# Memory-augmented attention in 64 dependent segments: column-tiled PV and P transposes, 4-byte block transposes, re-cut Wo rows, and 20 streamed weight pieces in place of 21

## The chip, the cores and the metric

One core of one Trainium2 chip. The metric is the device time of one execution in microseconds (us), as the median of several runs. Every profiled and timed run in this document was in the fast state; the granted TensorE clock, averaged over a run, was 0.98 to 0.99 in all of them. These averages are not as alike as they look; the section on the result says why.

## The reference, cut to what matters

```python
# S=2048, Dm=640, H=32 heads, Dh=192, M=8 memory rows, seg_len=32 -> 64 segments
def attention(x, mem0, Wq, Wk, Wv, Wo):
    mask = (idx[:, None] < M) | (idx[:, None] >= idx[None, :])       # 40 x 40
    mem = mem0
    for s in range(64):
        h = concat([mem, x[:, 32*s:32*s+32]], axis=1)                # 40 rows
        q, k, v = (einsum('btd,dhe->bhte', h, W) for W in (Wq, Wk, Wv))
        p = softmax(where(mask, q @ k.T * Dh**-0.5, -1e9))
        o = einsum('bhte,hed->btd', p @ v, Wo)
        mem = o[:, :M]                     # the next segment starts from it
        outs.append(o[:, M:])

b   = (gelu(x @ w_gate) * (x @ w_up)) @ w_down
g   = sigmoid((x * gate_w).sum(-1, keepdims=True))
out = g * a + (1 - g) * b                  # a: the attention's output
```

The eight memory rows make the 64 segments a chain. Nothing of segment s + 1 that touches the memory can start before the last Wo product of segment s is done. All of Wq, Wk, Wv and Wo (84 pieces in this kernel) is used in every segment.

## The kernel before

The FFN and the projections of the last 8 rows of each segment's input ("left") are done first, in some 316 us. Then come 64 segments. A segment works through four octets of eight heads. The program below is TensorE's order: `q`, `k`, `v` are projections (five pieces each), `sc` scores, `ex` the softmax on ScalarE and VectorE, `pt` the transpose of P, `pv` P times V, `wo` the output projection, `tq` and `tk` block transposes of Q and K on VectorE.

```python
PROG = [("q", 0), ("tq", 0), ("k", 0), ("tk", 0), ("v", 0),
        ("q", 1), ("sc", 0), ("tq", 1), ("k", 1), ("ex", 0), ("tk", 1), ("v", 1),
        ("q", 2), ("pt", 0), ("sc", 1), ("tq", 2), ("k", 2), ("ex", 1), ("tk", 2), ("pv", 0), ("v", 2),
        ("q", 3), ("pt", 1), ("sc", 2), ("tq", 3), ("ex", 2), ("k", 3), ("tk", 3), ("pv", 1), ("v", 3),
        ("pt", 2), ("sc", 3), ("pw", 0), ("ex", 3), ("wo", 0), ("pv", 2), ("pw", 1), ("wo", 1, 0), ("pt", 3),
        ("wo", 1, 1), ("wo", 1, 2), ("pv", 3), ("wo", 2), ("wo", 3)]
```

The weights do not all fit on chip. A Q, K or V piece has 384 KB (3072 bytes a partition), a Wo piece 320 KB. Two pieces are held in PSUM, most are resident in SBUF, and the rest is **streamed again in every segment** through five buffers. SyncE issues the loads in order; each waits until the buffer it goes into has been consumed. Which pieces stream is chosen so that they are spread evenly over the segment, by a cost model of TensorE's time:

```python
nstream = 0
while True:
    streamed = set()
    for k in range(nstream):
        target = (k + 0.5) * tseg / nstream
        best = min((i for i in range(npieces) if i not in streamed and i not in held_i), key=lambda i: abs(tcons[i] - target))
        streamed.add(best)
    if tot_bytes - GO - GQ - sum(piece_size(order[i]) for i in streamed) <= res_cap:
        break                                    # ends at 21 here
    nstream += 1
```

The operations that the change and the argument touch:

```python
def cmode(s, m, o, bank):                        # q, k: 5 pieces x 4 matmuls, 128x32 column tiles
    ...
    act: activation(out=rows_sb[m], in_=ps[:, bank, 0:384], func=Copy)            # rows evac
def row_transp(s, m, o):
    dve: transpose(out=dst[:, :, 0:L], in_=rows_sb[m])                            # 384 2-byte elements
def v_oct(s, o):
    left = s % 4 == 0                            # every 4th segment also makes Vl for four segments
    ...
def softmax(s, o):
    ...                                          # exp (ScalarE), sum and reciprocal (VectorE), then P:
    dve: tensor_tensor(out=pm_sb, in0=S3[:, :, 0:L], in1=rcb, op=mult)
         tensor_tensor(out=pl_sb[:, :, M*q:M*q+M], in0=S3[:, :, L:R], in1=rcb, op=mult)
def p_transp(s, o):                              # two full-width transposes
def pv_oct(s, o):
    pe: pair(A, 0, W, 0, 0, 1) + pair(A, W, W, 256, 1, 2)     # 4 full-width (128x128) matmuls
    pe: 4 matmuls in 64-column tiles                          # the middle chunk
    act: uT evac (two chunks)      dve: uT mid (one chunk)
def segment(s):
    ...                                          # PROG, then the hand-over:
    dve: mrow = ps[OB]                           # mem rows
    dve: rowb = ps[OB] * gate + rowb             # mix
    pe:  memT (6 matmuls)          dve: mem evac          # next segment may start
```

## Time and profile before

| | before |
|---|---|
| time, median of the first 3 runs | 1992.56 us (1985.2 to 1994.85) |
| profiled run | 1984.8 us |
| TensorE busy, of the span | 92% |
| DMA packet time per engine in an ordinary segment | 24.3 us of 25.14, 0.967 |
| period of a segment: Vl (s % 4 = 0) / ordinary (1, 2) / the one before Vl (3) | 26.79 / 25.14 / 25.73 us |

The periods are distances between the memory transposes of one segment and the next, read from the start times of all matmuls in the trace and averaged over 62 periods. The packet time is the sum of the durations of all DMA packets in these periods over 16 engines. The prediction shows the sums and windows behind the last rows. What it doesn't show are the lines that the experiments came to turn on. First two groups of the page (busy us, mean ns of one | idle time before): the ScalarE eviction of Q and K rows and VectorE's transpose behind it.

```profile
L929 DVE STREAM_TRANSPOSE arena<-arena 128x384 bf16<-128x384 bf16 x512 | 292.4, 571 | 136.1 <-ACT arena L924 135.9
L924 ACT ACTIVATE arena<-ps 128x384 bf16<-128x384 f32 x512 | 250.7, 490 | 308.3 <-PE ps L920 258.1
```

Then the waits view (who waits, on what: us in all, times, longest). TensorE's weight loads at the Q/K projections and at the P transposes wait for VectorE's product that makes P (L1002): 54 us over all lines. Waits for the stream are of the same size, 67 us, most of them for Q; those for Wo are a small part.

```profile
PEld ps L920 <- DMA arena<-in_A_Wq_dram: 35.8, 77, 1.4
...
PEld ps L920 <- DVE arena L1002: 26.0, 46, 2.2
PEld ps L1010 <- DVE arena L1002: 17.6, 39, 1.0
...
PEld ps L1064 <- DMA arena<-in_A_Wo_dram: 9.5, 23, 1.5
```

The first row for L1002 is written at a projection, which does not read P. I count it to the P transpose, which stands next in TensorE's program: in the start times the wait is a gap ahead of the last matmul of a Q block: 0.10 us in the third, 0.27 in the fourth, with 0.05 elsewhere some 0.45 us in an ordinary segment.

Last, TensorE's timeline at the start of segment 0, where V waits for the left half of x:

```profile
328.66 3.07 PE L939 MATMUL ps<-arena 128*32 128x384 bf16 x36 [9.97 <-DMA arena<-left_xt_scratch]
```

### The profile page before, as it was taken

How to read it: one execution, taken by the hardware profiler on the slowest of the kernel's cores; microseconds unless marked ns; L12 is line 12 of the kernel's file. 1: busy time of each engine (PE TensorE's matmuls, PEld its weight loads, DVE VectorE, ACT ScalarE, POOL GpSimd, SP SyncE). 2: the span in 40 equal slices, each digit the busy share in tenths (PEclk: the TensorE clock that was granted, in tenths of full speed). 3: DMA queues.
4: the chain of work that ended last, by engine and by line, in shares of the span. 5: the costliest groups of instructions: out<-in, count | busy, mean ns of one | idle time of the engine just before them, and what ended most of it. 6: DMA issues, size and time to landing. Idle time of an engine off the chain costs nothing.

```text
span 1984.8 us, 74702 instructions
## 1 busy us (share of the span) xinstructions
PE 1833.7 (92%) x32125; PEld 1092.4 (55%) x32125; DVE 1052.9 (53%) x3210; ACT 804.2 (41%) x1917; POOL 146.5 (7%) x547
## 2 busy tenths in 40 slices
PE   7899994899999999999999999999999999999998
PEld 3454442555565555555555555555555555556555
DVE  3222332456565656555555565656555555556565
ACT  2222221344444444444444444444444444444444
POOL 0000000000000000000000000000000000000000
PEclk9999996999999999999999999999999999999999
DMA  9411468999999999999998999999999999999998
GB/s 370 162 46 60 130 155 279 315 311 318 322 312 322 316 327 313 316 317 323 310 330 288 322 312 317 311 327 309 315 311 323 314 320 313 313 324 318 328 312 284
DMA packets 356327, 576.27 MB, mean 290 GB/s; under 512 B 83474, under 2 KB 240666, under 8 KB 355994
## 3 DMA queue, kind: packets, MB, share of 16 engines
q1 hardware_dynamic: 276922, 531.99, 79.8%
q10 hardware_dynamic: 79072, 39.50, 7.2%
q8 instruction: 251, 4.11, 0.8%
q14 instruction: 82, 0.67, 0.1%
HBM read 550.25 MB, written 21.10 MB: 288 GB/s over the span
## 4 chain that ended last, share of the span: by engine, by line
PE 73%; DMA 14%; DVE 5%; ACTq 5%; ACT 2%; issue 2%; SPq 0%; DVEq 0%
PE ps L1064 20%; PE ps L920 18%; PE ps L939 10%; DMA arena<-in_A_Wq_dram 5%; PE ps L842 4%; PE ps L968 3%; DMA arena<-in_A_Wo_dram 3%; PE ps L775 3%; PE ps L772 3%; PE ps L1030 2%; DMA arena<-in_A_Wk_dram 2%; PE ps L1044 2%; PE ps L960 2%; ACTq L666 2%; ACTq L857 2%; PE ps L790 2%
## 5 line engine op out<-in xcount | busy, mean ns | idle before, releaser
L920 PE MATMUL ps<-arena 128*32 128x384 bf16 x10240 | 527.0, 329 | 53.0 <-DVE arena L1123 21.2
L1064 PE MATMUL ps<-arena 128*40 128x320 bf16 x6144 | 466.6, 300 | 4.8 <-DMA arena<-in_A_Wo_dram 3.9
L924 ACT ACTIVATE arena<-ps 128x384 bf16<-128x384 f32 x512 | 250.7, 490 | 308.3 <-PE ps L920 258.1
L920 PEld LDWEIGHTS ps<-arena 128*32 128x32 bf16 x10240 | 252.4, 96 | 222.4 <-DMA arena<-in_A_Wq_dram 35.8
L929 DVE STREAM_TRANSPOSE arena<-arena 128x384 bf16<-128x384 bf16 x512 | 292.4, 571 | 136.1 <-ACT arena L924 135.9
L1064 PEld LDWEIGHTS ps<-arena 128*40 128x40 bf16 x6144 | 297.5, 100 | 102.9 <-DMA arena<-in_A_Wo_dram 9.5
L939 PE MATMUL ps<-arena 128*32 128x384 bf16 x6400 | 318.2, 329 | 12.4 <-DMA arena<-left_xt_scratch 10.0
L939 PEld LDWEIGHTS ps<-arena 128*32 128x32 bf16 x6400 | 162.7, 97 | 110.3 <-DMA arena<-left_xt_scratch 10.4
L599 ACT ACTIVATE arena<-ps 128x576 bf16<-128x576 bf16 (+1 forms) x192 | 114.3, 595 | 224.6 <-PE ps L1064 197.5
L900 POOL COPY arena<-arena 128x96 bf16<-128x96 bf16 x256 | 69.0, 270 | 1618.3 <-PE ps L968 851.6
L950 ACT ACTIVATE arena<-ps 128x384 bf16<-128x384 f32 x256 | 125.8, 492 | 133.8 <-PE ps L939 98.9
L1048 ACT ACTIVATE arena<-ps 128x320 bf16<-128x320 f32 x256 | 111.8, 437 | 130.2 <-PE ps L1032 130.1
L997 DVE TENSOR_REDUCE arena<-ps 104x4 f32<-104x160 f32 x256 | 82.1, 321 | 146.4 <-ACT ps L995 146.2
L1013 DVE TENSOR_TENSOR arena<-ps,arena 128x320 bf16<-128x320 bf16 x256 | 124.6, 487 | 35.5 <-PE ps L1011 30.7
L1108 DVE CAST arena<-ps 104x320 bf16<-104x320 f32 x63 | 31.0, 492 | 190.1 <-PE ps L1064 190.1
L995 ACT ACTIVATE ps<-ps 104x160 f32<-104x160 f32 x256 | 73.4, 287 | 118.5 <-DVE ps L985 77.2
L968 PE MATMUL ps<-arena 128*40 128x40 bf16 (+1 forms) x4096 | 120.7, 181 | 0.4
L612 ACT ACTIVATE arena<-ps 128x256 bf16<-128x256 bf16 x320 | 102.2, 386 | 36.5 <-DVE arena L1016 14.0
L1052 DVE CAST arena<-ps 128x160 bf16<-128x160 f32 x256 | 77.8, 304 | 72.1 <-PE ps L1044 69.1
L983 DVE TENSOR_REDUCE arena<-ps 104x4 f32<-104x160 f32 x256 | 80.8, 316 | 60.3 <-PE ps L968 60.0
L842 PE MATMUL ps<-arena 128*128 128x512 bf16 x480 | 104.3, 379 | 2.8 <-ACT arena L849 2.8
L968 PEld LDWEIGHTS ps<-arena 128*40 128x40 bf16 (+1 forms) x4096 | 99.2, 96 | 11.4 <-DVE arena L929 2.0
(75 smaller groups left out, 1702.5 us busy)
## 6 DMA issues: line engine op xcount, KB each, us to landing
arena<-in_A_Wo_dram SPq DMA_DIRECT2D x528, 320.0 KB, 4.5
arena<-in_A_Wk_dram SPq DMA_DIRECT2D x404, 384.0 KB, 4.7
arena<-in_A_Wq_dram SPq DMA_DIRECT2D x341, 384.0 KB, 4.5
arena<-in_A_Wv_dram SPq DMA_DIRECT2D x146, 384.0 KB, 5.0
left_qk_scratch<-arena ACTq DMA_DIRECT2D x16, 768.0 KB, 7.9
arena<-left_qk_scratch ACTq DMA_DIRECT2D x64, 192.0 KB, 4.7
arena<-in_A_x_dram SPq DMA_DIRECT2D x4, 640.0 KB, 15.2
xt_scratch<-arena ACTq DMA_DIRECT2D x4, 640.0 KB, 9.1
```

Source lines behind the costliest of these rows:

```text
L599: S_.add("act", lambda e: e.activation(out=bview(o_held2, GQ)[:, c0:c1], in_=psb(b)[:, p0:p0 + c1 - c0], func=ACTF.Copy), reads=[r_ps[b]], ...
L612: S_.add("act", lambda e, b=b: e.activation(out=flat[:, 256 * b:256 * b + 256], in_=psb(b)[:, 768:1024], func=ACTF.Copy), reads=[r_ps[b]], ...
L842: S_.add("pe", [lambda e, k=k, g_=gs[k][0], i=i, bk=bk: e.matmul(ps[:, bk, 0:NL].rearrange("p (g t) -> p g t", t=L), g_[:, i * 128:(i + 1) ...
L920: S_.add("pe", [lambda e, j=j, k=k, gv=gv: e.matmul(ps[32 * j:32 * j + 32, bank, 0:384].rearrange("p (c i) -> p c i", i=32), Hb[hb][:, k, ...
L924: S_.add("act", lambda e: e.activation(out=rows_sb[m], in_=ps[:, bank, 0:384], func=ACTF.Copy), reads=[r_ps[bank]], writes=[r_rows[m]], na ...
L929: S_.add("dve", lambda e: e.transpose(out=dst[:, :, 0:L], in_=rows_sb[m].rearrange("p (c r) -> p c r", r=L)), reads=[r_rows[m]], writes=[r ...
L939: return [lambda e, j=j: e.matmul(ps[32 * j:32 * j + 32, bk, 0:384], lhs, g_[:, 384 * j:384 * (j + 1)], start=(k == 0), stop=(k == KT - 1) ...
L950: S_.add("act", lambda e: e.activation(out=v_sb[o % NVB], in_=ps[:, bank, 0:384], func=ACTF.Copy), reads=[r_ps[bank]], writes=[r_v[o % NVB ...
L968: fns.append(lambda e, gp=gp, lo=lo, hi=hi, i=3 * tl + c, tl=tl, last=(c == 1): e.matmul(ps[gp:gp + R, bank, tl * R:(tl + 1) * R], Qs[lo:h ...
L1013: S_.add("dve", lambda e: e.tensor_tensor(out=PTm, in0=apx(pv[:, 0:104], [[64, 2], [0, 4], [1, R]]), in1=apx(mbd, [[0, 2], [1, 4], [0, R]] ...
L1048: S_.add("act", lambda e: e.activation(out=apx(u[:, 0, 0, :], [[2 * R, 2], [3 * R, 4], [1, R]]), in_=ps[:, A, 0:2 * W].rearrange("p (c t r ...
L1064: fns.append(lambda e, g_=g_, i=i, c=c, h=h, tl=tl, cc=cc, u=u: e.matmul(ps[64 * h:64 * h + R, OB, 0:HD], u[:, tl, cc, :], g_[:, i, HD * h ...
```

## The change

Its intent is to shorten both things that run near full: fewer streamed bytes in larger packets for the DMA engines, and fewer changes of tiling for TensorE. VectorE is relieved along the way. The diff, cut to its core:

```diff
-    wsA["rowb"] = al(HD * 2)
-    wsA["mrow"] = al(HD * 2)                      # 1280 bytes a partition freed ...
+    o_rowb, o_mrow = wsB_off["v"] + 768, wsB_off["v"]   # ... by overlaying both on the V buffers
 # Wo rows by threes: a partition's two rows are adjacent in DRAM unless p % 3 == 1
-            return Wo2[:, 2 * key[1]:2 * key[1] + 2, :]
+            r0, r1 = wo_row(2 * key[1]), wo_row(2 * key[1] + 1)      # wo_row(c) = 384*(c//3) + c%3
+            return bass.AP(Wo2.tensor, Wo2.offset + r0 * Dm, [[3 * Dm, 128], [(r1 - r0) * Dm, 2], [1, Dm]])
+    def may_stream(key):
+        return key[1] % 3 != 1 if key[0] == 3 else key[0] != 2 or key[1] >= 2
 # exp is put ahead of the next k block (PROG), COST gets new numbers, tseg = tt + 1.4
 # Q/K rows: pairs of 2-byte elements, transposed as 4-byte ones
-        act: activation(out=rows_sb[m], in_=ps[:, bank, 0:384], func=Copy)
+        act: activation(out=rows_sb[m].rearrange("p (b i h) -> p b h i", b=6, h=2), in_=..., func=Copy)
-        dve: transpose(out=dst[:, :, 0:L], in_=rows_sb[m])
+        dve: transpose(out=dst[:, :, 0:L], in_=rows_sb[m].bitcast(F32))
 # Vl of octets 0 and 1 is made at the end of the segment before
-        left = s % 4 == 0
+        left = s % 4 == 0 and (s == 0 or o >= 2)
 # P in one product for octets 0 to 2; P transposes in column tiles
-        dve: pm_sb = S3[:, :, 0:L] * rcb ; pl_sb[..] = S3[:, :, L:R] * rcb
+        dve: p_sb[0:104, :, 0:R] = S3 * rcb                        # o < 3; o = 3 as before
+        pe:  8 transposes in 32-column tiles (o < 3), 4 in 64-column tiles (o = 3)
 # PV
-        pe: pair(A, 0, W, 0, 0, 1) + pair(A, W, W, 256, 1, 2)      # full width
+        pe: for cc in 3 chunks, for left in (False, True), for h in 2 halves: one 64-column tile
-        dve: uT mid
+        act: uT mid (o < 2)      dve: uT mid (o >= 2)
 # hand-over
-        mem rows, mix, memT, mem evac
+        mem rows, [Vl of o0 ahead], memT, [Vl of o1 ahead], mem evac, mix      # [..] if (s+1) % 4 == 0
 # b_load moves from k2 to behind the last pv (its buffer is V's now);
 # the eight gate copies move from ScalarE's DMA queue, late, to SyncE's, early
```

The mask is now two 64x64 tiles and the scores begin with the 64-row ones. The selection loop ends with 20 streamed pieces, 8 of Wo and 12 of Q, K and V.

> **What bounds the kernel now.** I read the sums of the page first, then the chain of waits for the period of a segment, then windows of single segments, then TensorE's timeline in two segments.
>
> The page, busy tenths in 40 slices: TensorE and the DMA engines are both nearly full from the eighth slice on, so no single row decides.
> ```profile
> PE 1833.7 (92%) x32125; PEld 1092.4 (55%) x32125; DVE 1052.9 (53%) x3210; ACT 804.2 (41%) x1917; POOL 146.5 (7%) x547
> ...
> PE   7899994899999999999999999999999999999998
> ...
> DMA  9411468999999999999998999999999999999998
> ...
> q1 hardware_dynamic: 276922, 531.99, 79.8%
> ```
> Some 316 us are the FFN, the left projections and set-up; the rest is 64 dependent segments. The memory transpose (L1119) marks each end. Its 63 groups run from 364.9 to 1957.5 us: 62 periods, 25.69 us each. The chain of waits gives the single starts: most segments take 24.5 to 25.6 us, every fourth (the one that also projects Vl) 26.7. Segment 0 takes 49.8 us.
>
> Windows (columns: length, busy time of PE, weight loads, DVE, ACT, POOL, granted clock, DMA share, GB/s): the first is a Vl segment, the next two ordinary ones, the last two lie in segment 0.
> ```profile
> 955.00:981.00 26.00, 25.20 (x518) 15.96 (x510) 16.51 (x51) 11.31 (x28) 2.15 (x8) 1.00 0.93 304
> ...
> 981.15:1005.77 24.62, 23.32 (x454) 14.29 (x454) 14.62 (x47) 11.45 (x28) 2.16 (x8) 1.00 0.98 331
> ...
> 1005.77:1030.57 24.80, 23.51 (x454) 14.33 (x454) 14.73 (x47) 11.19 (x28) 2.16 (x8) 1.00 0.97 326
> ...
> 316.00:328.50 12.50, 2.70 (x45) 1.25 (x44) 1.16 (x2) 2.45 (x5) 0.00 (x0) 0.64 0.82 263
> 328.50:340.00 11.50, 10.63 (x190) 5.88 (x194) 4.17 (x13) 3.93 (x7) 1.44 (x6) 0.73 0.64 215
> ```
> The ordinary segment is bound by DMA (0.97 to 0.98). The Vl segment is bound by TensorE: its timeline has hardly a gap. Vl is four times 20 matmuls at 0.82 us, 3.28 us, so TensorE alone needs 26.7 - 3.3 = 23.4 us for an ordinary segment and loses 1.3 to 2.2 us there. The cause is the stream: counts of the DMA issues give (1419 weight issues - 75 at the start) / 64 = 21 pieces a segment, 8 of Wo and 13 of Q, K, V.
>
> TensorE's timeline of one ordinary segment (start, duration; I count from start to start):
> ```profile
> 1004.94 0.47 PE L1119 MATMUL ps<-arena 128*128 128x8 bf16 x6 [0.59 <-DVE arena L1108]
> 1005.77 1.81 PE L920 MATMUL ps<-arena 128*32 128x384 bf16 x40 [0.36 <-DVE arena L1123]
> 1007.41 0.99 PE L939 MATMUL ps<-arena 128*32 128x384 bf16 x20
> 1008.22 0.99 PE L920 MATMUL ps<-arena 128*32 128x384 bf16 x20
> 1009.13 0.25 PE L960 MATMUL ps<-arena 128*40 128x160 bf16 x2
> 1009.22 0.46 PE L968 MATMUL ps<-arena 128*40 128x40 bf16 x16
> 1009.61 1.00 PE L920 MATMUL ps<-arena 128*32 128x384 bf16 x20
> ...
> 1025.28 0.24 PE L1030 MATMUL ps<-arena 128*128 128x160 bf16 x1
> ...
> 1025.58 0.29 PE L1044 MATMUL ps<-arena 128*64 128x160 bf16 x4
> 1025.70 1.52 PE L1064 MATMUL ps<-arena 128*40 128x320 bf16 x20
> ```
> A Q block takes 0.82 us ahead of another 32-column block and 0.91 ahead of the mask: a change of the array's tiling costs about 0.1 us. The segment hand-over idles TensorE 0.59 + 0.36 = 0.95 us.
>
> **What the Trainium skill says.** TensorEngine Tiling (Array Packing), Key Properties: changing the tiling mode drains TensorE. The 0.1 us above agrees. TensorE: Matmul & The Clock Gate, part 1: starts of small matmuls are never closer than about 25 ns. The 16 score matmuls take 0.39 us, 24 ns each: agrees. DMA: Bandwidth & Descriptors, Why small descriptors are slow: a fixed cost per packet. In the trace's packet records a 1280-byte packet takes 63.1 ns (mean), a 3072-byte one 142.9: 50.5 against 47.6 ns per KB, so it agrees but is small. Vector Engine (DVE) Microarchitecture Reference, 3.8: the 32x32 transpose passes one element per cycle per lane. The trace can't show its 4-byte case yet; its VectorE evictions of 160 and 384 elements took 304 and 544 ns, 1.07 ns an element, and the 384-element transpose 571 ns, so a pace of one element at a time fits.
>
> **The change, part by part.**
>
> (1) *Streamed bytes.* The 1280 bytes per partition of the b and memory rows are freed and let one more Q/K/V piece stay: by the selection loop's arithmetic 20 pieces, 8 of Wo and 12 of Q, K, V. One piece is 128 packets x 142.9 ns / 16 engines = 1.14 us. Wo rows by threes make the two rows that a partition gets adjacent for all pieces allowed to stream, so 256 packets of 1280 bytes become 128 of 2560. By a line through the two means a 2560-byte packet takes 120 ns, against 2 x 63.1 = 126: 8 x 128 x 6 / 16 = 0.39 us. All packets between 420 and 1950 us took 1460.5 us per engine; over 59.6 periods that is 24.5 us a segment. After: 24.5 - 1.14 - 0.39 = 23.0 us. At the share that an ordinary segment reaches now (0.97) it needs **23.7 us**.
>
> (2) *TensorE in a segment.* PV now: beside the 32-column blocks 0.1 in, 0.30 for the four full-width matmuls with a switch, 0.12 for the four tiled ones, 0.1 out, 0.62; beside Wo 0.1 + 0.30 + 0.12 = 0.52 (Wo has the same tiles). After: three groups like the tiled one, 0.36, with 0.1 + 0.1 beside the blocks and none beside Wo. Saved 2 x 0.06 + 2 x 0.16 = 0.44 us. P transposes 0 to 2: a drain less (0.1), but eight small ones at 25 ns in place of two take 0.1 more: nothing. The last P transpose, beside Wo: 0.1 + 0.19 becomes four at 25 ns: 0.19 saved. The reordered scores let the last octet pass to Wo without a switch: 0.1. Sum 0.73: an ordinary segment needs **22.7 us** of TensorE.
>
> (3) *Vl for octets 0 and 1 ahead.* 1.64 us leave the Vl segment and go to the end of the segment before, where they fill 0.95 us of hand-over. So TensorE needs 22.7 + 1.64 = **24.3** in the Vl segment and 22.7 + 0.69 = **23.4** in the one before.
>
> (4) *VectorE and ScalarE.* A 4-byte transpose has 192 elements fewer: 571 - 192 x 1.07 = 366 ns, 8 x 0.2 = 1.6 us saved. Joined P products: 3 x (291 + 181 - 333) = 0.42 us. Two mid evictions of 304 ns go to ScalarE, which has 13 us free. VectorE falls from 14.7 to some 12.1 us. All lies beside other work; only the waits for the P product (L1002: about 15 us of PE idle in all, mostly inside DMA slack) shrink.
>
> (5) *Segment 0.* V waited 10 us for the left x load, which sat in ScalarE's queue behind the eight gate copies (9.5 us). These move to SyncE's queue, long before. But that segment also loads late residents: the windows of its 50 us add up to 43 us of DMA at full share. So I take 6 us of the 10.
>
> (6) *Set-up otherwise* (mask halves, zeroing, later memory load): under 1 us on the path.
>
> Sum: of four segments, two ordinary at 23.7, the Vl one at 24.4, the one before it at 23.9 (both bounds near each other cost a little): mean 23.9 against 25.69. 63 x 1.79 = 113 us, plus 6: 1992.6 - 119 = 1873. I put the prediction at **1872 us**.
>
> **The rivals.** *A: the overlays become waits.* The b rows may be loaded only after the last PV (some 4.9 us before the segment's end), and ScalarE must first evict and issue (0.44 + 0.8 us); the load took 4.6 us to land. So it lands about 1 us after the end, and the mix sits in VectorE's queue ahead of the next Q transpose, due 1.6 us after the start. For: there is no room to spare. Likewise V's second eviction must wait for the out stores (issued 2 to 3.6 us into the segment, 4.0 us to land), 1 to 2 us later than now. Against: both have 1 to 3 us until TensorE needs them. If they bite, 0.3 to 0.6 us a segment: about 1900. *B: the DMA is limited by bytes alone.* If larger packets gain nothing the ordinary segment needs 24.1: mean 24.2, 1893. For: the rate per byte differs only 6% between sizes. *C: the strided reads are slow.* The V weights now step three elements and Q/K two. If weight loads there took twice their 100 ns, PV would save nothing; TensorE would have 23.1, still under the DMA: about 1880. *D: better than summed.* With TensorE further from binding, queues refill sooner, share 0.99 and 0.2 us less PE: mean 23.3, 1835.
>
> **Range and chances.** The path gets shorter in every part and both bounds fall by 5 to 6% or more, so less than 2% (over 1952.7) would need new waits of over 1.2 us a segment. Range 1838 to 1915. Faster 0.94, within 2% 0.05, slower 0.01.
>
> **What would show it right or wrong.** Right: 20 pieces a segment, packets of 2560 bytes near 120 ns; period near 23.9 us with DMA share still 0.96 to 0.97 in ordinary segments; the Vl segment within 1 us of the others; PV beside Wo 0.36 us from start to start; transpose near 366 ns; no left-x wait in segment 0, which takes about 44 us. Wrong: TensorE waiting for the Q or K transpose behind the mix, ScalarE waiting for the out stores with TensorE behind it, the DMA share well under 0.95 (then TensorE or a hand-over binds), or transposes no shorter.

## The result, and the profile after

**1904.35 us** (median of 4 runs, 1898.99 to 1909.86) against 1992.56 (1993.7 with the fourth run of the kernel before, 2001.03, counted in). The ratio is 0.9553 with a 95% interval of 0.9501 to 0.9606: faster. Ratios here are the mean time of one kernel's fast runs over that of the other's of the same rounds, so not quite the ratio of the medians. The prediction was 1872 with a range of 1838 to 1915: in the range, but the gain was 89 us where 120 had been predicted. The profiled runs took 1907.2 and 1984.8 us.

The rows of the page after that answer to those of before: TensorE busy is down 72 us, the DMA row is hardly less full, the weight queue moves 26 MB less.

```profile
PE 1762.1 (92%) x34421; PEld 1126.8 (59%) x34429; DVE 929.6 (49%) x2890; ACT 874.6 (46%) x2045; POOL 145.1 (8%) x547
...
DMA  9511567999999998999999999999999999999998
...
q1 hardware_dynamic: 201386, 506.45, 77.6%
```

Windows of three segments, an ordinary one, a Vl one and an ordinary one (columns as in the prediction):

```profile
1240.63:1265.15 24.52, 22.45 (x490) 14.70 (x491) 12.81 (x42) 12.46 (x31) 2.14 (x8) 1.00 0.95 322
...
1312.60:1337.47 24.87, 24.19 (x555) 17.23 (x551) 14.69 (x46) 11.98 (x30) 2.14 (x8) 1.00 0.92 303
1337.47:1362.32 24.85, 22.01 (x491) 14.51 (x491) 12.80 (x42) 12.41 (x31) 2.14 (x8) 1.00 0.94 323
```

The ordinary segment has lost over a us of TensorE work and 1.8 us of VectorE's, but only 0.9 us of length, and the share of the DMA engines has fallen to 0.94 to 0.95: **now neither is full**. Over all periods:

| mean period, us | Vl | ordinary | before Vl | mean of all | DMA share, ordinary |
|---|---|---|---|---|---|
| before | 26.79 | 25.14 | 25.73 | 25.68 | 0.967 |
| predicted | 24.4 | 23.7 | 23.9 | 23.9 | 0.97 |
| after | 25.43 | 24.26 | 24.62 | 24.63 | 0.946 |
| after, only periods at full clock | 25.43 | 24.08 | 24.28 | | |

Segment 0 ends at 352.8 us, 12.2 earlier than before. With 63 times (25.68 - 24.63) = 66 us that makes 78, the difference of the two profiled runs.

The last row of the table is about the granted clock. Within the 62 periods the trace of the kernel after has eight stretches of 3.4 us in which TensorE was granted half its clock, that of the kernel before has one. One of the eight periods hit (columns as above; the granted clock is the 0.94):

```profile
477.13:503.54 26.41, 23.83 (x491) 15.34 (x491) 12.62 (x42) 12.40 (x31) 2.14 (x8) 0.94 0.89 291
```

Four ordinary periods were hit, with 25.49 us on average, and four before a Vl segment, with 25.58. Against the periods at full clock that is some 11 us in all, a loss that no step of the prediction has. All eight stretches begin 0.5 to 1.8 us after a memory transpose. Count the 62 periods in steps of 3.41 us, on whose grid this record changes: there are 447. In the eight steps just ahead of a stretch TensorE was busy 0.40 to 0.60 of the time, in the other 439 it was busy 0.62 or more. So a late Wo piece and the hand-over behind it seem to cost a second time, at half clock. No run tests this by itself, and the limit is not sharp everywhere: in place20 below, two steps with 0.45 and 0.50 were not followed by a stretch.

TensorE's timeline at the end of an ordinary segment (start, duration; a group's duration runs past the next start, so count from start to start):

```profile
1353.79 0.49 PE L1071 MATMUL ps<-arena 128*64 128x160 bf16 x12
1354.11 0.71 PE L1094 MATMUL ps<-arena 128*40 128x320 bf16 x8
1354.66 0.26 PE L1045 MATMUL ps<-arena 104*64 104x104 bf16 x4
1354.75 1.25 PE L1094 MATMUL ps<-arena 128*40 128x320 bf16 x16
...
1359.72 2.00 PE L1094 MATMUL ps<-arena 128*40 128x320 bf16 x25 [1.77 <-DMA arena<-in_A_Wo_dram]
1362.32 0.47 PE L1149 MATMUL ps<-arena 128*128 128x8 bf16 x6 [0.59 <-DVE arena L1139]
```

PV beside Wo takes 0.32 us (0.52 before), the last P transpose 0.09: TensorE's own sums hold. But the last Wo block stops for 1.77 us here, because a piece of Wo has not landed. (This is a long one; the mean at this place is 0.46 us.) The hand-over ahead of a Vl segment, on the other hand, is filled with Vl (L975) as meant, with no idle time:

```profile
1311.67 1.00 PE L975 MATMUL ps<-arena 128*32 128x384 bf16 x20
1312.60 0.47 PE L1149 MATMUL ps<-arena 128*128 128x8 bf16 x6
1313.00 1.00 PE L975 MATMUL ps<-arena 128*32 128x384 bf16 x20
```

The two groups again. The transpose has become 200 ns shorter and the eviction ahead of it, which now writes every second 2-byte element, 119 ns longer:

```profile
L935 ACT ACTIVATE arena<-ps 128x384 bf16<-128x384 f32 x512 | 311.6, 609 | 148.6 <-PE ps L931 130.4
...
L941 DVE STREAM_TRANSPOSE arena<-arena 128x192 f32<-128x192 f32 x512 | 190.1, 371 | 120.8 <-ACT arena L935 120.2
```

The waits have changed places: those for the P product (L1027 now) have nearly gone. Those for Wo are seven times as long as before and those for Q less than half; over all pieces the weight loads wait 103 us for the stream, where they waited 67. The two overlays show as waits of ScalarE and VectorE:

```profile
PEld ps L1094 <- DMA arena<-in_A_Wo_dram: 65.7, 124, 2.1
ACT arena L962 <- DMA out_dram<-arena: 47.5, 38, 2.4
...
PEld ps L931 <- DMA arena<-in_A_Wq_dram: 15.3, 23, 3.2
...
DVE arena L1160 <- DMA arena<-ffn_b_scratch: 8.7, 10, 3.2
PEld ps L951 <- DVE arena L1027: 4.9, 19, 0.3
...
PEld ps L1045 <- DVE arena L1027: 2.7, 10, 0.6
```

In segment 0 V follows without a wait:

```profile
319.75 2.58 PE L951 MATMUL ps<-arena 128*32 128x384 bf16 x40
```

### The profile page after: what moved, and what is told of

Its sections match the earlier page's. It is cut to its first block, busy times and chain, and to the rows that moved or that the text cites. A ratio compares the mean times of both kernels' runs of the same rounds, so it can differ in the third digit from the quotient of the medians.

```text
span 1907.2 us, 78849 instructions
## 1 busy us (share of the span) xinstructions
PE 1762.1 (92%) x34421; PEld 1126.8 (59%) x34429; DVE 929.6 (49%) x2890; ACT 874.6 (46%) x2045; POOL 145.1 (8%) x547
## 4 chain that ended last, share of the span: by engine, by line
PE 66%; DMA 24%; DVE 4%; ACTq 3%; issue 1%; ACT 1%; SPq 0%; DVEq 0%
PE ps L931 19%; DMA arena<-in_A_Wo_dram 13%; PE ps L1094 11%; PE ps L951 11%; DMA arena<-in_A_Wv_dram 5%; PE ps L852 4%; PE ps L1071 4%; DMA arena<-in_A_Wq_dram 4%; PE ps L993 3%; PE ps L785 3%; PE ps L782 3%; ACTq L867 2%; DMA arena<-in_A_Wk_dram 2%; PE ps L800 2%; PE ps L985 2%; PE ps L975 1%
## 5 line engine op out<-in xcount | busy, mean ns | idle before, releaser
L931 PE MATMUL ps<-arena 128*32 128x384 bf16 x10240 | 516.5, 334 | 29.2 <-DVE arena L1154 16.3
L1094 PE MATMUL ps<-arena 128*40 128x320 bf16 x6144 | 479.8, 300 | 30.6 <-DMA arena<-in_A_Wo_dram 26.3
L1094 PEld LDWEIGHTS ps<-arena 128*40 128x40 bf16 x6144 | 308.1, 100 | 135.8 <-DMA arena<-in_A_Wo_dram 65.7
L935 ACT ACTIVATE arena<-ps 128x384 bf16<-128x384 f32 x512 | 311.6, 609 | 148.6 <-PE ps L931 130.4
L931 PEld LDWEIGHTS ps<-arena 128*32 128x32 bf16 x10240 | 254.7, 98 | 173.1 <-DVE arena L1154 20.8
L951 PE MATMUL ps<-arena 128*32 128x384 bf16 x5800 | 294.6, 332 | 4.0 <-DMA arena<-in_A_Wv_dram 3.0
L941 DVE STREAM_TRANSPOSE arena<-arena 128x192 f32<-128x192 f32 x512 | 190.1, 371 | 120.8 <-ACT arena L935 120.2
L951 PEld LDWEIGHTS ps<-arena 128*32 128x32 bf16 x5800 | 147.6, 98 | 93.5 <-DMA arena<-in_A_Wv_dram 9.1
L962 ACT ACTIVATE arena<-ps 128x384 bf16<-128x384 f32 x256 | 125.6, 491 | 161.6 <-PE ps L951 79.5
L1071 PEld LDWEIGHTS ps<-arena 128*64 128x64 bf16 x3072 | 113.0, 125 | 59.3 <-DVE ps L1010 25.8
L1071 PE MATMUL ps<-arena 128*64 128x160 bf16 (+1 forms) x3072 | 136.4, 222 | 7.7 <-ACT arena L623 3.5
L993 PE MATMUL ps<-arena 64*40 64x40 bf16 (+1 forms) x4096 | 120.6, 181 | 1.9 <-issue 1.7
L993 PEld LDWEIGHTS ps<-arena 64*40 64x40 bf16 (+1 forms) x4096 | 100.2, 97 | 11.5 <-issue 2.6
```

The costliest lines, as they stand in the source:

```text
L931: S_.add("pe", [lambda e, j=j, k=k, gv=gv: e.matmul(ps[32 * j:32 * j + 32, bank, 0:384].rearrange("p (c i) -> p c i", i=32), Hb[hb][:, k, ...
L935: S_.add("act", lambda e: e.activation(out=rows_sb[m].rearrange("p (b i h) -> p b h i", b=6, h=2), in_=ps[:, bank, 0:384].rearrange("p (b ...
L941: S_.add("dve", lambda e: e.transpose(out=dst[:, :, 0:L], in_=rows_sb[m].bitcast(F32).rearrange("p (c r) -> p c r", r=L)), reads=[r_rows[m ...
L951: return [lambda e, j=j: e.matmul(ps[32 * j:32 * j + 32, bk, 0:384], lhs, g_[:, 384 * j:384 * (j + 1)], start=(k == 0), stop=(k == KT - 1) ...
L962: S_.add("act", lambda e: e.activation(out=v_sb[o % NVB], in_=ps[:, bank, 0:384], func=ACTF.Copy), reads=[r_ps[bank]], writes=[r_v[o % NVB ...
L993: fns.append(lambda e, gp=gp, lo=lo, hi=hi, b=(3 * tl + c) // 2, h=(3 * tl + c) % 2, tl=tl, last=(c != 1): e.matmul(ps[gp:gp + R, bank, tl ...
```

## The experiments

Three questions: what sets the length of a segment now, where did the expected 30 us go, and which parts of the change bring the gain. Theories in the texts on record: the **stream** sets the segment (S), in one of two ways, through the rate of the DMA engines or through the five **buffers**, of which one comes free too late for its load to land in time (B); or **TensorE** does, with its waits for other engines (T). Each call was timed against the kernel before in the same rounds (medians of before 1994.16, 1995.31 and 1995.47 us, 7 runs each). Where I give a difference to the kernel after, it is the difference of the two ratios times 1995 us. The kernel after itself was timed in the first round alone, with an interval of 10 us to each side. Put together with the interval of the other run, such a difference is known to within 11 to 13 us only: 76, 49 and 24 us are clear of that, 17, 13 and 12 barely, and "no difference" means none of more than some 12.

The granted clock differs too. Of the 62 periods, those with a half-clock stretch are: after 8, wo1280 10, vlinplace 7, gateact 6, place20 and twobyte 4, pvfull and placeheld 3, vecold and before20 2, before 1, ring6, alias16 and before6 none. So means over all periods mix two things, and I add those of the periods at full clock where the reading turns on them.

Several kernels give a wrong result on purpose: where a weight piece is read in place of another ("alias"), the operations, shapes and times of the engines stay, and only the load or the space of the piece goes.

### Four of the 20 streamed pieces not loaded (alias16; wrong result on purpose)

```diff
+    ALIAS = {(0, 1, 1): (0, 1, 0), (1, 2, 1): (1, 2, 0), (2, 3, 0): (2, 2, 1), (3, 8): (3, 7)}
+    streamed -= {order.index(k) for k in ALIAS}
     ...
+        key = ALIAS.get(key, key)         # in piece() and left_piece()
```

> The changed kernel with four of its 20 streamed pieces no longer loaded: their matmuls read a resident piece instead, so the result is wrong on purpose and the work of every engine is the same. It measures what the stream costs. Theory S (the stream still sets the period; TensorE alone would need 22.4 us in an ordinary segment, 24.2 in the one with Vl, mean 22.9): period 22.9 to 23.1 instead of 24.63, so 63 x 1.6 = about 100 us less than the changed kernel, near 1803; the waits for Wo transfers gone. Theory H (new hand-over waits of the overlays keep TensorE back): less than 40 us gained, over 1860.

1829.19 us (1824.64 to 1832.19), ratio 0.9171 [0.9151, 0.9191]: 76 us less than the kernel after. An ordinary segment takes 22.80 us and the waits for Wo are gone:

```profile
1217.43:1240.21 22.78, 21.88 (x491) 15.67 (x491) 12.62 (x42) 12.59 (x31) 2.15 (x8) 1.00 0.86 274
```
```profile
PEld ps L1099 <- DMA arena<-in_A_Wo_dram: 1.2, 4, 0.5
```

So in the kernel after the stream costs 24.26 - 22.80 = 1.46 us of an ordinary segment (1.28 against its periods at full clock), and TensorE with all its other waits needs 22.80, close to the 22.7 of the prediction. I had expected some 1803 us in all. The floor is higher in every kind of segment: 22.80 us for 22.4 in the ordinary one, 24.98 for 24.2 in the Vl one, 23.24 in the one before it. The Vl segment takes its 24.98 us with hardly a wait for the stream, 0.58 us over the 24.4 of the prediction's sum.

### Another choice of 20 pieces (place20; correct)

```diff
+    streamed = {(0,0,2),(1,0,4),(0,1,1),(1,1,0),(1,1,4),(0,2,3),(1,2,1),(2,2,0),(0,3,1),(1,3,0),
+                (1,3,4),(2,3,3),(3,0),(3,3),(3,6),(3,11),(3,12),(3,17),(3,21),(3,23)}
     # after: ... (2,3,0),(2,3,4),(3,2),(3,5),(3,8),(3,11),(3,15),(3,18),(3,21),(3,23)
```

> The changed kernel with another choice of which 20 pieces are streamed (still 8 of Wo and 12 of Q, K and V, the same bytes), so that any five streamed pieces in a row lie at least 4.8 us of TensorE time apart; now the last Wo piece comes only 4.4 us after the piece whose buffer it takes, while a transfer takes 4.5 us from issue to landing. Theory P (the place of the pieces, with five buffers, is what keeps the DMA share at 0.945 instead of 0.97): the wait before the last Wo piece (0.46 us in 31 of 32 ordinary segments) falls below 0.2, the period by 0.3 to 0.4 us, 20 to 25 us in all, near 1880. Rival R (the rate of the DMA alone): the wait moves to other pieces and the time stays within 8 us.

1898.89 us, ratio 0.9516 [0.9476, 0.9555]: 7 us less than after, and the intervals overlap, so inconclusive. The mechanism moved as meant: the gap before the last streamed Wo piece fell from 0.46 to 0.26 us an ordinary segment. But waits for Wo stay at 41.3 us where 65.7 were: with five buffers, relief at one place came back partly at others.

### Wo loaded in 1280-byte packets again (wo1280; wrong result on purpose)

```diff
-            return bass.AP(Wo2.tensor, Wo2.offset + r0 * Dm, [[3 * Dm, 128], [(r1 - r0) * Dm, 2], [1, Dm]])
+            return bass.AP(Wo2.tensor, Wo2.offset + 256 * key[1] * Dm, [[Dm, 128], [128 * Dm, 2], [1, Dm]])
```

> The changed kernel with Wo loaded in the old row order: 256 packets of 1280 bytes a piece again instead of 128 of 2560; the same pieces, the same places (wrong result on purpose, the rows no longer fit). Packets measured so far: 63.1 ns for 1280 bytes, 122.9 for 2560, so the long packets save 8 x 128 x 3.3 / 16 = 0.2 us of DMA a segment. If the DMA rate sets the period: 10 to 16 us slower than the changed kernel. If the latency of the last pieces counts more, up to 25. If packets don't matter: within 4 us.

1922.27 us, ratio 0.9636 [0.9597, 0.9675]: **17 us** more than after, barely clear of the noise. It is within what was expected, but the two traces don't show that the packets did it. The packet time of an ordinary segment is 0.23 us longer, as reckoned; its period at full clock is not (24.01 us against 24.08). Of the 10 us between the two profiled runs, 3.5 lie ahead of the end of segment 0 and nearly all the rest in the periods at half clock, ten here and eight there. So what larger packets are worth is not settled. A 2560-byte packet takes 122.9 ns on average in the kernel after, two of 1280 bytes took 126.2 before.

### PV in its old form (pvfull; wrong result on purpose)

```diff
+        S_.add("pe", pair(A, 0, W, 0, 0, 1) + pair(A, W, W, 256, 1, 2), ...)      # full width
+        ...                                                                     # 4 matmuls in 64-column tiles
-        for cc, bank, c0 in ((0, A, 0), (1, A, W), (2, B, 0)): ...              # 12 in 64-column tiles
```

> The changed kernel with PV in its old form, four full-width matmuls and four tiled ones an octet instead of twelve tiled ones (wrong result on purpose, the rows of Wo no longer fit). My step gave the tiled form 0.44 us of TensorE a segment. Theory S (the stream sets the period): nearly all of it is hidden, the time is 0 to 10 us longer than the changed kernel's. Rival (TensorE sets it): 63 x 0.44 = 28 us longer.

1904.76 us, ratio 0.955 [0.9517, 0.9583]: **no difference** to after (0.9553), where the rival expected 28 us. TensorE's best case for a segment (the 10th percentile of each item, summed) is 22.74 us here and 22.4 in the kernel after: PV did get 0.3 us shorter, and it is hidden: nothing of it is seen in the time.

### Six buffers in place of five, the same 20 pieces (ring6; wrong result on purpose)

```diff
-    B_RING = int(opts.get("ring", 5))
+    B_RING = int(opts.get("ring", 6))
+    ALIAS = {(3, 7): (3, 4), (3, 17): (3, 14)}      # two resident pieces give the space
```

> The changed kernel with six stream buffers in place of five, and the same 20 pieces streamed at the same places; the room comes from two resident Wo pieces that are read from others' buffers (wrong result on purpose). Theory B (five buffers are too few to hide the 4.5 to 5 us from issue to landing while TensorE uses pieces unevenly; the DMA engines idle in mid-segment with all buffers full): the DMA share of ordinary segments rises from 0.945 to 0.965 or more, their period falls from 24.25 to 23.7 or less, the wait before the last Wo piece goes under 0.15 us; 25 to 45 us in all, near 1870. Rival R (the rate alone): within 8 us of the changed kernel.

1857.12 us (1848.71 to 1863.43), ratio 0.9305 [0.9271, 0.9338]: **49 us less** than after, with the same bytes streamed.

```profile
1204.36:1227.21 22.85, 21.83 (x490) 15.08 (x490) 12.82 (x42) 12.29 (x31) 2.14 (x8) 1.00 0.97 331
```
```profile
PEld ps L1097 <- DMA arena<-in_A_Wo_dram: 6.6, 15, 0.8
```

An ordinary segment takes 23.11 us, 1.15 of the 1.46 us that alias16 says the stream costs (0.97 of 1.28 at full clock; the rest is the half-clock stretches, of which both runs have none). The DMA engines are at 0.963, and TensorE's weight loads wait 15 us for the stream in place of 103. So the engines can deliver this stream in 23.1 us; in the kernel after they stand idle for part of the segment because all five buffers are full, and are late afterwards. This decides for the buffers and against the rate.

### The kernel before with 20 pieces (before20; one weight piece replaced on purpose)

```diff
 # before.py
+    ALIAS = {(1, 2, 3): (1, 2, 2)}
+    streamed -= {order.index(k) for k in ALIAS}
```

> The kernel before with one of its 21 streamed pieces not loaded (its matmuls read a resident piece: wrong result on purpose), so 20 pieces of 8 Wo and 12 Q, K, V, all else as before. It tells the part of the gain that one piece less gives by itself. A piece is 1.14 us of DMA a segment; ordinary segments have 24.3 us of packets now and a TensorE need of 23.4. Theory S: ordinary segments fall by 0.8 to 1.0 us, the Vl segments (26.8, TensorE) stay: 46 x 0.9 = about 40 us less than before, near 1953, nearly half of the whole gain of 89. Rival T (the gain comes from TensorE's shorter work): under 15 us less.

1984.77 us, ratio 0.9953 [0.9926, 0.998]: 9 us less than before, where the stream theory expected some 40. (The result passed the tolerance although one K piece was wrong.) So **one piece less is nearly worthless to the kernel before**. Its ordinary segment shrank only from 25.14 to 25.00 us. The waits view says what came in its place:

```profile
PEld ps L925 <- DVE arena L1007: 38.4, 57, 1.9
```

That is the wait for the P product that had 26.0 us in the kernel before. By the start times TensorE waits 0.76 us for it in an ordinary segment, 0.45 before. And with five buffers the stream itself was relieved only in part: the weight loads still wait 43 us for it, where they waited 67.

### The kernel before with six buffers (before6; wrong result on purpose)

```diff
 # before.py
+    B_RING = 6;  ALIAS = {(3, 7): (3, 5), (3, 17): (3, 14)};  nstream = 21
```

> The kernel before with six stream buffers and its 21 pieces (room from two resident Wo pieces read from others' buffers: wrong result on purpose). If the DMA rate bound its ordinary segments, as I predicted from the share of 0.97: within 8 us of the kernel before. If it was five buffers together with the wait for VectorE's P product: the stream waits (0.6 us a segment by position) go, the waits for the P product grow to some 0.7 us; 15 to 30 us less than before, ordinary segments near 24.7, not near TensorE's 23.4.

1965.47 us, ratio 0.9843 [0.9828, 0.9858]: 31 us less than before with all 21 pieces. The share of the DMA engines in ordinary segments rises from 0.967 to 0.973 at 24.84 us. The weight loads' waits for the stream fall from 67 to 6 us. So the rate did not bind in the kernel before either, although its share of 0.97 to 0.98 looked like it. TensorE's waits for the P product rise to some 0.9 us a segment: relieved of the stream, the kernel before waits for VectorE.

### VectorE's work put back in the kernel after (vecold; correct)

```diff
-            fns = [p_sb[0:104, :, 0:R] = S3 * rcb]
+            fns = [p_sb[.., 0:L] = S3[:, :, 0:L] * rcb,  p_sb[.., L:R] = S3[:, :, L:R] * rcb]
-        on_act = o < NOCT - 2
+        on_act = False
     # and PROG with ("ex", o) at its old places
```

> The changed kernel with three of its VectorE savings undone, correct results: the P product in two instructions in every octet, the mid eviction of PV always on VectorE, and the exponentials in the old places of the program; the 4-byte transposes stay. Theory V (in the kernel before, TensorE waited in ordinary segments for the P product: 54 us of weight loads and 15 us of matmuls behind it, about 0.45 us a segment by position; the changed kernel has 8 and 0.2): the wait for the P product comes back in part, 0.15 to 0.4 us a segment, 8 to 25 us slower than the changed kernel. My prediction's step (VectorE's work lies beside other work): within 5 us.

1931.55 us, ratio 0.9674 [0.9659, 0.9688]: **24 us** more than after. The wait is back:

```profile
PEld ps L931 <- DVE arena L1028: 37.2, 65, 0.8
```

The kernel after has no such row above its noise (L951 and L1045, shown above, hold 7.6 us together). The earlier `exp`, the joined product and the two mid evictions on ScalarE are thus the largest single part of the change that these runs could isolate. They were not separated from one another. At full clock the ordinary segment takes 24.48 us against 24.08.

### Block transposes of 2-byte elements again (twobyte; correct)

```diff
-            out=rows_sb[m].rearrange("p (b i h) -> p b h i", b=6, h=2), in_=...        # and the 4-byte views
+            out=rows_sb[m], in_=ps[:, bank, 0:384]
```

> The changed kernel with the Q and K block transposes in 2-byte elements again, with the layouts that go with it, correct results: VectorE gets 8 x 0.2 us a segment back, ScalarE's row evictions fall from 609 to 490 ns, weights of the scores are read without a step. Theory V (VectorE's chain from scores to P is one of the bounds that the change relieved): 5 to 20 us slower than the changed kernel, with waits of TensorE for the P product. Rival (the transposes lie beside other work): within 5 us, or a little faster for ScalarE's shorter evictions.

1903.28 us, ratio 0.9537 [0.9504, 0.957]: no difference. VectorE's transpose gains 200 ns and the eviction on the same chain loses 119. That both lie beside TensorE work otherwise fits, but is not shown apart.

### Vl of octets 0 and 1 back in its own segment (vlinplace; correct)

```diff
-        left = s % 4 == 0 and (s == 0 or o >= 2)
+        left = s % 4 == 0
-            ahead = (s + 1) % 4 == 0
+            ahead = False
```

> The changed kernel with the Vl products of octets 0 and 1 back in their own segment. My step: 1.64 us of TensorE go back into the Vl segment, which then needs 24.2 + 1.64 = 25.8 to 26.3 against 25.4 now, and the hand-over before it has its 0.95 us gap again, hidden or not. If each Vl segment was TensorE's: 16 x 0.5 to 0.9 = 8 to 14 us slower than the changed kernel. If the stream hides it: within 4 us.

1919.33 us, ratio 0.9616 [0.9589, 0.9643]: **13 us** more than after, barely clear of the noise. The Vl segment goes from 25.43 to 26.83 us and the one before it from 24.62 to 23.94. By these means Vl ahead gave 1.40 and took 0.68, as the prediction had it (0.69). But three of the fifteen Vl segments here, and four of the segments before them in the kernel after, were at half clock. At full clock it is 26.47 against 25.43 and 23.88 against 24.28: Vl ahead gave 1.04 us, well short of TensorE's 1.64, and took 0.40.

### Gate copies back on ScalarE's queue (gateact; correct)

```diff
-            S_.add("sp", lambda e: e.dma_start(gseg[..], gcol[..]), ...)      # before the late residents
+            aux_dma(gseg[..], gcol[..], ...)                                  # ScalarE, just ahead of the left x load
```

> The changed kernel with the eight gate copies back in ScalarE's queue, just before the left x load of segment 0. The start up to the end of segment 0 took 352.8 us in the changed kernel and 364.9 before. If the wait for left x (10 us before) is what went: it comes back, 8 to 12 us slower. If segment 0 is bound by its loads, as I reckoned: about 6 us slower. If the gain at the start came from elsewhere: under 3.

1912.61 us, ratio 0.9577 [0.9549, 0.9606]: 5 us more than after, within the noise, so the size is not settled. The wait in segment 0 is back, shorter than the 9.97 us of before, and the segment ends at 355.8 us in place of 352.8:

```profile
323.68 3.07 PE L950 MATMUL ps<-arena 128*32 128x384 bf16 x36 [3.41 <-DMA arena<-left_xt_scratch]
```

So the queue of the gate copies accounts for 3.4 us of waiting where the prediction put 6 to 10. The end of the segment doesn't confirm even these: place20 and wo1280, which keep the copies early, end it at 355.4 and 356.3 us. The clock differs here as well: between 290 us and the end of segment 0, TensorE was at half clock for 34.1 us in the kernel after and in wo1280, for 37.5 in place20 and for 41.0 in gateact. Where the rest of the 12 us that segment 0 gained comes from stays open.

### place20 with the held copies re-ordered (placeheld; correct)

```diff
     # place20, and in held_copy: the early parts are the banks that PV of octet 2 needs first
+            held_early[0] = [(misc[0] + 3) % 5, (misc[0] + 4) % 5]
     # out_store(s - 1) behind q0 in place of k0
```

> A version meant to beat both, correct results: the changed kernel with the other choice of the 20 streamed pieces (one look at it gave 24.39 us a segment against 24.63), the early part of the held Wo piece taken from the two PSUM banks that PV of octet 2 does not write next (TensorE waited 14 us for these copies), and the out stores issued after the Q block, not the K block. Placing alone about 10 us, the banks 8 to 10 us, mostly in Vl segments, the stores nothing: 1880 to 1890.

1897.16 us (1889.57 to 1903.95), ratio 0.9491 [0.9467, 0.9514], the lowest time of a correct kernel, some 12 us under after at the face of the ratios. Its interval overlaps after's and place20's, and the Vl segment, at which it aimed, did not shorten (25.58 us). Most of it is probably place20's 7 us; it isn't shown to be more.

## Why the prediction was right, and where it was not

The verdict, faster, was right, and the time lay in the range, 32 us above the point and 11 under the upper end. That it lay there in spite of the step that failed below is partly luck: the segments alone missed by 45 us, and only the wide range and a start that gained 6 us more than reckoned took that up.

**What held.** The number of streamed pieces (20). The packet time of a segment, predicted 23.0 us, measured 23.0 (mean of all 62 periods), with 122.9 ns for a 2560-byte packet (120). TensorE's best case: 22.4 us ordinary and 24.2 Vl, against 22.7 and 24.3 (before Vl 22.5, where 23.4 had been put). PV beside Wo, 0.32 us (0.36). The transpose, 371 ns (366). The left-x wait of segment 0 gone; the segment ends 12 us earlier where 6 had been put, though not all for that reason. Not so good: the Vl segment is 1.17 us longer than the ordinary one, where "within 1 us" had been put. And the 25 ns that part (2) puts for a small matmul is only a mean (16 score matmuls in 0.39 us): in the trace of the kernel before, these start in pairs 2 to 4 ns apart, most pairs 22 to 26 ns after the one before, one some 110 ns. A sentence that took this mean for the least distance has been cut from the text on record.

**The step that failed** is this: "At the share that an ordinary segment reaches now (0.97) it needs 23.7 us." The share did not stay. It fell to 0.946, and the ordinary segment took 24.26 us. (The prediction named a share well under 0.95 as a sign of being wrong, but put it down to TensorE or a hand-over.) The step took a share near 1 for a rate limit and scaled it with the bytes. Ring6 and before6 refute the limit: the same bytes through six buffers take 49 and 31 us less, and TensorE hardly waits for them. The limit was the depth of the ring. A load can start only when the piece five places earlier has been consumed, and takes 4.5 us (Wo) or some 5 us (Q, K, V) from issue to landing, the medians of the page. By the kernel's own cost model the last streamed Wo piece, p23, can start 4.4 us before it is needed (p8, five places ahead, is consumed at 16.26, p23 at 20.66). That is an estimate from the model, and it agrees with the trace: that piece is late in 31 of 32 ordinary segments, by 0.46 us on average. A faster TensorE shortens that window and leaves the landing time as it is.

**The size of it.** By the table of periods, the misses are 0.56 us for each of two ordinary segments, 1.03 for the Vl one, 0.72 for the one before it: on average 0.72, times 63 = 45 us too little. The start gave 6 us more than predicted. 1872 + 45 - 6 = 1911, against 1907.2 in the profile. Some 11 of the 45 us lie in the eight periods with a half-clock stretch; at full clock the ordinary segment missed by 0.38 us and the one before Vl by as much. For the ordinary segment the cause of that is shown (ring6). Of the Vl segment's 1.03 us, 0.58 remains even with four loads less (alias16). In its timeline PV of octet 2 stands behind ScalarE's held copies, but placeheld's attempt on these did not shorten it, so that cause is not settled.

**A second step failed in size**: "All lies beside other work; only the waits for the P product ... shrink." These waits were taken for slack inside a segment bound by DMA. Since DMA did not bind, they cost time: putting the old VectorE work back costs 24 us. In the kernel before, TensorE waited for the ring (67 us of weight loads) and for VectorE's product (54), and the two covered each other in part. Before6 shows it: with the waits for the stream down to 6 us, those for the product rose to 80, and the gain was 31 us. Before20 took away less of the stream's waits (to 43) and gained 9. No run relieved VectorE alone in the kernel before. The change relieved VectorE's product and the bytes at once, which fits its gain of 89 but is not shown to be the reason.

**TensorE's savings in PV were right and worth nothing** that these runs could see: PV's 0.3 us a segment is in the trace, and taking it back does not change the time (pvfull).

**The rivals.** A, the overlays: both waits came, 47.5 us of ScalarE for the out stores and 8.7 us of VectorE for the b rows. They were absorbed: alias16 has 65.0 us of the first and still runs its ordinary segments in 22.80 us. B, bytes alone: its time (1893) is near the result, but it too had the rate bind, which ring6 refutes; whether larger packets gain anything is not settled (wo1280). C, strided reads: weight loads of PV took 125 ns where the tiled ones before took 108, not twice as long, and without effect. D, better than summed, with a share of 0.99: the opposite happened, a faster TensorE did not refill the queues sooner because there were no free buffers to refill.

**Where the 89 us come from**, by the runs that take one part away, each known to within some 12 us: VectorE's product 24, packets 17 (not confirmed by the traces), Vl ahead 13, gate copies about 5, PV and the 4-byte transposes 0; the streamed piece less was worth 9 in the kernel before. These sum to 68. They need not sum to 89, since parts that relieve different limits can be worth more together than one by one. The half-clock stretches took some 8 us back (11 in the kernel after, 3 in the one before), and I have no run that splits the rest.

## What to carry to other kernels

A DMA share of 0.97 does not prove that the rate binds. Two cheap kernels settle it even with a wrong result: leave some loads out, and give the ring one buffer more at the same bytes; then compare, for the piece that comes late, the time from the release of its buffer to its use with the time from issue to landing. Where two waits cover each other, relieving one alone can show next to nothing (9 us here), so look at the waits by their place in the period, and count waits of a nearly full engine as free only after the other limit has been shown to bind. Before comparing mean periods, look at the granted clock of each period: eight of 62 were hit here, and the mean of the segments before Vl moved by 0.34 us with them.

## What the Trainium skill lacked or had wrong

- "DMA: Bandwidth & Descriptors", Anatomy of one DMA: it gives a DMA as some 2.0 us plus bytes over 436 GB/s (fitted on the GpSimd path), which makes 2.9 us of a 384 KB load. Here, issued from SyncE with up to five in flight, it took 5.1 us at the median, 4.5 for 320 KB. The page has no word on how many buffers a stream then needs; one more brought 49 us here, and 31 in the kernel before.
- The same page, Why small descriptors are slow: it calls joining descriptors "only worth it at ≤256 B desc size". Here 1280-byte packets took 50.5 ns per KB, 2560-byte ones 49.2, 3072-byte ones 46.9 (after). So joining still shortens the packets above 256 bytes, by a little; the time of the kernel with 1280-byte packets on two fifths of the pieces was 17 us longer of 1922, which the traces don't tie to the packets.
- "ScalarE: Activation LUTs", What ACT_TABLE_LOAD costs: 186 ns + 0.833 ns an element for an activation with immediate scale and bias. The eviction of 384 elements agrees where it writes them in a row (490 ns; the formula gives 506), but that section gives no time for stepped output: writing every second 2-byte element took 609 ns.
- "TensorEngine Tiling (Array Packing)", Key Properties: it has the drain at a change of tiling, but no size. Here it cost about 0.1 us each time, and PV without it got 0.3 us a segment shorter.
- No page gives a time for weight loads from every third element: 125 ns here for 64 columns, against 108 for adjacent ones, with no effect on the time.
- No page gives the busy share of TensorE at which its clock is halved. In the kernel after, eight steps of 3.41 us with TensorE busy 0.40 to 0.60 were each followed by one at half clock, and none of the 439 steps with 0.62 or more.
